# A rebuilt attention stage ahead of a branched expert stage, with the first two conditional blocks prepared before the branch

## The chip, the cores and the metric

The kernel runs on one core of a Trainium2 chip. The metric is the device time of one launch in microseconds (us). The kernel before takes 843.26 us, the median of three runs (842.16 to 844.25). All arithmetic is fp32.

## What is computed

Two parts are chained. The first is cross attention between a sequence and a small state, in both directions; the second sends each row of the result through one of eight experts, the one whose embedding it is closest to.

```python
# x: (8, 8, 512, 64), state: (8, 8, 32, 64)       B, H, S, D and Ns = 32
scores = scale * x @ state.T                      # softmax over the 32 states
xread  = softmax(scores) @ state                  # 512 rows a head
scores2 = scale * state @ x.T                     # softmax over the 512 positions
sread  = softmax(scores2) @ x                     # 32 rows a head
rows = concat(xread, sread) as (8*544, 8*64)      # N = 4352 rows of D = 512
xn, en = rows / |rows|, emb / |emb|
logits = xn @ en.T / tau                          # 8 experts
e, gate = argmax(logits), softmax(logits)[argmax]
out = gate * relu(rows @ w1[e]) @ w2[e]           # w1: 512x1024, w2: 1024x512
```

## The kernel before, in words

**Attention stage.** A *unit* is one batch `b` and one half `g` of its heads (four heads), 16 units in all, numbered `u = 2b + g`. `states(b)` puts the state of a batch block-diagonally into `bdst` (four copies on POOL), transposes it on PE (`st_ps`), copies it to `bd` and multiplies it with the normalised expert embeddings (`pj_ps`), so that eight extra columns of `bdst` give the router's logits along with the read. `scores(u)` transposes `x` on PE (`xt_ps`, eight 128x128 blocks), multiplies it with the state twice: once as `sT_ps` (states on the partitions, 512 positions along the row; for the softmax over positions) and once as `s_ps` (positions on the partitions; for the softmax over states). The first softmax makes `e2` and a diagonal matrix `dg` of reciprocal sums, the second makes `e1`. `reads(u)` transposes `e1` (`a_ps`) to `aT`, multiplies `e2` by `dg` while it turns it (`e_ps`) to `a2`, and then makes the two reads, `x_ps` (from `aT`) and `sr_ps` (from `a2`). `rows(b)` writes the rows to DRAM (`x_rows`), adds the logits, squares the rows for their norm (four `junk` activations a batch), and `choose` finds the expert. After each four batches `state_rows` does the same for the state rows (`xst_ps`, `lg_ps`). In the loop over units, `scores(u+1)` stands ahead of `reads(u)`.

The loads of `x` (1 MB a batch, in pieces of 256 bytes, four issues of 256 KB) and of the first expert weights `w1` (2 MB each, all eight kept in `w1_sb`), and the writes of the rows, are all issued by SP. A load of `x` for batch `b+2` waits until the two buffers' older batch is read.

**Routing.** Counts, ranks and destinations of the rows are worked out on DVE and with some matmuls (`rk_ps`, `inv_ps`), 207 to 243 us. The result is a table of blocks of 128 rows of one expert each.

**Expert stage.** `run(a, z)` goes over the blocks `j`: `gather` (POOL, an indirect load of 128 rows), `turn_x` (PE transposes to `xT`), `hidden` (PE with `w1`, relu to `h`), `turn_h` (`hT`), `result` (PE with `w2`, scaled by the gate to `y`, an indirect store by POOL). `load_w2` is issued by SP. There are always 34 blocks; up to 41 can be needed, by the data. So `run(0, 34)` is followed by two nested branches, for blocks 34 to 36 and 37 to 40. The count is read into a register of every engine. In these runs 37 blocks are used, so the first branch is entered and the second is not. Inside a branch `run` begins anew, with gathers, transposes and first weights.

**What sets the order.** A scheduler orders the instructions of each engine when the program is built, by priorities that follow the code and its own estimate of when each is ready; on the chip each engine runs its list in that order, one after the other.

The few lines that set the order of the units are

```python
ready = {0: scores(0, 0, x_nat[0], st[0][1])}
for u, (b, g) in enumerate(units):
    ...
    if u + 1 < len(units):
        ready[u + 1] = scores(b1, g1, x_nat[b1], st[b1][1])
    reads(b, g, x_nat[b], st[b][0], xr[b], *ready.pop(u))
```

## Time and profile before

| what | us |
|---|---|
| median of three runs | 843.26 |
| the profiled execution, its own time | 844.45 |
| its span, first to last instruction | 842.4 |
| attention stage, span 0 to the end of the last `sr_ps` | 206.8 |
| routing, to the first `h_ps` | 206.8 to 253.8 |
| 34 blocks, to the end of the last `y_ps` ahead of the branch | 253.8 to 771.3 |
| PE without work at the branch | 771.3 to 781.2 |
| three conditional blocks and the end | 781.2 to 842.4 |

Engines are PE (matmul), PEld (its weight load, which overlaps), DVE, ACT, POOL and SP. A group of instructions is named by its line, the tile it writes and the tiles it reads. An fp32 matmul appears as two instructions, an fp32 transpose as one; so `sT_ps` x4 is two matmuls. PE is busy for 91% of the span, DVE for 27%, ACT for 16% and POOL for 14%, but these are averages over a stage in which DVE and ACT work most of the time (attention) and one in which they mostly wait (experts).

### The profile page before, as it was taken

The page shows a single profiled execution, that of the slowest core. Times are in us where ns is not written, and L with a number is a line of the kernel's source. Part 1 is how long each engine was busy: PE and PEld are TensorE (multiplying, and loading weights), DVE is VectorE, ACT ScalarE, POOL GpSimd, SP SyncE. Part 2 cuts the span into 40 slices and gives each one's busy share as a digit, 9 for nine tenths or more (in the row PEclk, how much of TensorE's full clock was granted, in tenths as well). Part 3 has the DMA queues.
Part 4 walks back from the last instruction along what each step waited for, and adds up shares of the span by engine and source line. Part 5 has one row for each costly group of instructions (what it writes and reads, how often), then busy time and mean ns, then how long its engine had stood idle before and what let it go on. Part 6 is the DMA issues. An engine that isn't in the chain of part 4 may idle for free.

```text
span 842.4 us, 8400 instructions
## 1 busy us (share of the span) xinstructions
PE 769.3 (91%) x3104; PEld 438.0 (52%) x3104; DVE 225.6 (27%) x499; ACT 133.7 (16%) x272; POOL 115.9 (14%) x184
## 2 busy tenths in 40 slices
PE   6899999998359999999999999999999999996994
PEld 4677767777244454454444544545445454442441
DVE  3455555555701111121121211212112111111111
ACT  3244444344100010000000000001000010000000
POOL 2011111101211101111111101111111110002000
PEclk9899999999559999999999999999999999999897
DMA  9486662242033464553644545546455464446130
GB/s 264 186 279 181 211 216 81 47 102 79 9 130 143 137 217 146 165 204 132 209 164 152 203 138 191 178 140 220 140 176 198 130 212 140 149 179 212 50 113 16
DMA packets 92753, 131.40 MB, mean 156 GB/s; under 512 B 37726, under 2 KB 45918, under 8 KB 92712
## 3 DMA queue, kind: packets, MB, share of 16 engines
q1 hardware_dynamic: 86760, 112.20, 41.3%
q0 software_dynamic: 5920, 18.62, 6.4%
q8 instruction: 27, 0.44, 0.2%
q14 instruction: 14, 0.11, 0.0%
q10 hardware_dynamic: 32, 0.02, 0.0%
HBM read 113.00 MB, written 18.61 MB: 156 GB/s over the span
## 4 chain that ended last, share of the span: by engine, by line
PE 82%; issue 7%; DVE 5%; DMA 2%; POOL 1%; ACT 1%; POOLq 0%; ACTq 0%; DVEq 0%
PE y_ps L516 28%; PE h_ps L490 28%; PE sT_ps L219 5%; PE ht_ps L509 3%; PE s_ps L224 3%; PE x_ps L271 3%; PE sr_ps L279 3%; PE xt_ps L479 2%; PE inv_ps L431 2%; PE e_ps L264 2%; DVE xT L70 1%; PE pj_ps L199 1%; DMA xin<-x_rows,src_row 1%; PE a_ps L259 1%; DMA x_rows<-xs 1%
## 5 line engine op out<-in xcount | busy, mean ns | idle before, releaser
L516 PE MATMUL y_ps<-w,hT 128*128 128x512 f32 x592 | 263.9, 599 | 1.1 <-ACT hT L68 0.8
L490 PE MATMUL h_ps<-w_sb,xT 128*128 x592 | 262.6, 597 | 0.0
L490 PEld LDWEIGHTS h_ps<-w_sb,xT 128*128 128x128 f32 x592 | 113.4, 192 | 142.6 <-issue 142.3
L516 PEld LDWEIGHTS y_ps<-w,hT 128*128 128x128 f32 x592 | 109.4, 190 | 129.2 <-issue 123.9
L498 ACT ACTIVATE h<-h_ps 128x512 f32<-128x512 f32 x37 | 22.1, 597 | 431.9 <-PE h_ps L490 431.9
L520 DVE TENSOR_SCALAR y<-y_ps,gpos 128x512 f32<-128x512 f32 x37 | 27.8, 751 | 227.8 <-PE y_ps L516 227.8
L500 DVE TENSOR_SCALAR h<-h_ps 128x512 f32<-128x512 f32 x37 | 25.6, 692 | 231.2 <-PE h_ps L490 231.2
L521 POOL DMA_INDIRECT out_dram<-y,dst_row x37 | 37.5, 1014 | 312.0 <-DVE y L520 304.7
L466 POOL DMA_INDIRECT xin<-x_rows,src_row x37 | 38.1, 1030 | 217.9 <-PE xt_ps L479 199.4
L219 PE MATMUL sT_ps<-xT,bd 128*128 128x512 f32 x64 | 39.4, 745 | 7.4 <-DVE xT L70 7.2
L509 PEld LDWEIGHTS ht_ps<-ident,h 128*128 128x128 f32 x296 | 34.6, 141 | 19.5 <-issue 19.5
L68 ACT ACTIVATE hT<-ht_ps 128x512 f32<-128x512 f32 x37 | 22.1, 597 | 129.9 <-PE ht_ps L509 129.9
L479 PE MATMUL xt_ps<-ident,xin 128*128 128x128 f32 x148 | 24.1, 290 | 20.3 <-DMA xin<-x_rows,src_row 20.3
L509 PE MATMUL ht_ps<-ident,h 128*128 128x128 f32 x296 | 38.4, 273 | 0.0
L224 PEld LDWEIGHTS s_ps<-bd,xT 128*128 128x128 f32 x256 | 32.0, 194 | 10.0 <-issue 10.0
L271 PE MATMUL x_ps<-bdst,aT 128*128 128x264 f32 x128 | 32.9, 401 | 0.0
L279 PEld LDWEIGHTS sr_ps<-xn,a 128*32 128x32 f32 x512 | 29.0, 110 | 5.5 <-DVE r L249 4.5
L279 PE MATMUL sr_ps<-xn,a 128*32 128x64 f32 x512 | 31.6, 220 | 0.0
L481 DVE COPY xT<-xt_ps 128x512 f32<-128x512 f32 x37 | 25.2, 682 | 21.6 <-PE xt_ps L479 21.6
L224 PE MATMUL s_ps<-bd,xT 128*128 128x64 f32 x256 | 30.5, 272 | 0.0
L479 PEld LDWEIGHTS xt_ps<-ident,xin 128*128 128x128 f32 x148 | 18.3, 150 | 22.0 <-DMA xin<-x_rows,src_row 11.4
L252 POOL TENSOR_TENSOR e<-e,r 128x512 f32<-128x512 f32 x16 | 16.8, 1048 | 78.3 <-DVE r L251 62.6
(128 smaller groups left out, 474.3 us busy)
## 6 DMA issues: line engine op xcount, KB each, us to landing
w<-in_moe_w_dram SPq DMA_DIRECT2D x37, 2048.0 KB, 10.1
w_sb<-in_moe_w_dram SPq DMA_DIRECT2D x8, 2048.0 KB, 9.4
xn<-in_x_dram SPq DMA_DIRECT2D x32, 256.0 KB, 4.1
x_rows<-xr SPq DMA_DIRECT2D x16, 512.0 KB, 5.5
xin<-x_rows,src_row POOLq DMA_INDIRECT x37, 3.7
out_dram<-y,dst_row POOLq DMA_INDIRECT x37, 7.8
...
```

The lines of the kernel that those rows point to most:

```text
L219: nc.tensor.matmul(sT, lhsT=bd[:, g, j], rhs=xT[:, j], start=(j == 0), stop=(j == 1))
L224: nc.tensor.matmul(s[:, c * P + j * half : c * P + j * half + half], lhsT=xT[:, j, c * P : c * P + P], rhs=bd[:, g, j, j * half : j * half ...
L271: nc.tensor.matmul(ps[:, 0:XW], lhsT=aT[:, c * P : c * P + P], rhs=bs[:, g], start=True, stop=True)
L279: nc.tensor.matmul(ps[q0 : q0 + Ns, i * Dh : i * Dh + Dh], lhsT=a2[:, c * P + i * Ns : c * P + i * Ns + Ns], rhs=xn[:, c, (HPG * g + i) * ...
L466: nc.gpsimd.indirect_dma_start(out=t, out_offset=None, in_=x_rows[:], in_offset=bass.IndirectOffsetOnAxis(ap=src_row[:, j : j + 1], axis=0 ...
L479: nc.tensor.transpose(ps[:, k * P : k * P + P], t[:, k * P : k * P + P], ident)
L490: nc.tensor.matmul(ps, lhsT=xT[:, k * P : k * P + P], rhs=w1f[:, ds(ek * (KD * F) + k * F + i * 512, 512)], start=(k == 0), stop=(k == KD ...
L500: nc.vector.tensor_scalar(dst, ps, 0.0, None, ALU.max)
L509: nc.tensor.transpose(ps[:, k * P : k * P + P], h[:, f0 : f0 + P], ident)
L516: nc.tensor.matmul(ps, lhsT=hT[:, k * P : k * P + P], rhs=w2[:, k], start=(k == 0), stop=(k == KF - 1))
L520: nc.vector.tensor_scalar(y, ps, gpos[:, j : j + 1], None, ALU.mult)
L521: ins = nc.gpsimd.indirect_dma_start(out=out[:], out_offset=bass.IndirectOffsetOnAxis(ap=dst_row[:, j : j + 1], axis=0), in_=y, in_offset= ...
```

## The change

The attention stage is rebuilt; eight things differ.

1. **State, prepared once.** The transposed states of all batches (`bd`, two tiles of four batches) and the products with the embeddings (`proj`) are made at the start, from two copies of the state that ten issues on ACT's queue load (1 MB together). `states(b)` then only issues four small loads of the state straight into `bdst` (SP) and copies `proj` (POOL).
2. **`sT_ps` in two halves.** Each matmul writes 64 of the 128 partitions, with 64 columns of `bd`.
3. **No `s_ps`.** The scores with positions on the partitions come from `sT_ps` by a DVE transpose of 32x32 blocks (`STREAM_TRANSPOSE`), the subtraction of the maximum moves from DVE to POOL.
4. **No `a_ps`.** `e1` is turned to `aT` by a second DVE transpose.
5. **`dg` is gone.** ACT scales `e2`, and `e_ps` is a plain transpose.
6. **Copies move to ACT:** `a2`, and all four `xr` copies of a unit.
7. **Order of the units.** `turn(u+2)` (the transposes of `x`) stands ahead of `reads(u)`, and `scores(u+2)` behind it. `x` of three batches is kept: the third buffer, `spare`, and one of the `bd` tiles lie in the space of the last expert's `w1`.
8. **The branch.** `run(0, 34)` also gathers and turns blocks 34 and 35 and hands the turned blocks to `run(34, 37, xT)`, which gathers only block 36 anew. The register read of the count stands ahead of `run(0, 34)` in the code.

The diff, without most of the start and the plain renamings:

```diff
         def load_x(b):
-            t = att.tile([P, NCH, D], FP32, tag="xn", name="xn")
+            if b % 3 == 2:
+                t = spare[:, 0 : NCH * D].rearrange("p (c d) -> p c d", c=NCH)
+            else:
+                t = att.tile([P, NCH, D], FP32, tag="xn", name="xn")
...
+        for b in range(B):
+            p0 = Ns * (b % 4)
+            nc.scalar.dma_start(st_row[p0 : p0 + Ns, b // 4], state[b].rearrange("h n d -> n h d"))
...
+            nc.scalar.dma_start(
+                st_nat[g], state[:, HPG * g : HPG * g + HPG].rearrange("b i n d -> (i n) b d")
+            )
         x_nat = {0: load_x(0)}
...
         nc.scalar.dma_start(emb, moe_expert_emb[:])
...
         x_nat[1] = load_x(1)
+        x_nat[2] = load_x(2)
...
         def states(b):
             bs = bdst[b % 2]
             for i in range(HPG):
-                nc.gpsimd.tensor_copy(
-                    bs[Ns * i : Ns * i + Ns, :, Dh * i : Dh * i + Dh], st_nat[Ns * i : Ns * i + Ns, b]
-                )
-            ps = bank("st_ps")
-            for g in range(HG):
-                for j in range(2):
-                    nc.tensor.transpose(
-                        ps[:, (2 * g + j) * P : (2 * g + j + 1) * P], bs[:, g, j * P : j * P + P], ident
-                    )
-            bd = att.tile([P, HG, 2, P], FP32, tag="bd", name="bd")
-            nc.scalar.activation(bd.rearrange("p g j n -> p (g j n)"), ps, AF.Copy)
-            pp = bank("pj_ps")
-            for g in range(HG):
-                for j in range(2):
-                    nc.tensor.matmul(
-                        pp[:, g * E : g * E + E], lhsT=bd[:, g, j], rhs=enT[:, 2 * g + j],
-                        start=(j == 0), stop=(j == 1),
-                    )
-            nc.vector.tensor_copy(
-                bs[:, :, GW:XW], pp[:, 0 : HG * E].rearrange("p (g e) -> p g e", e=E)
-            )
-            return bs, bd
-        def scores(b, g, xn, bd):
-            xT = att.tile([P, 2, S], FP32, tag="xT", name="xT")
+                nc.sync.dma_start(
+                    bs[Ns * i : Ns * i + Ns, :, Dh * i : Dh * i + Dh],
+                    state[b].rearrange("(g i) n d -> i n g d", g=HG)[i],
+                )
+            nc.gpsimd.tensor_copy(bs[:, :, GW:XW], proj[:, b])
+            return bs
+        def turn(b, g, xn):
+            xT = [att.tile([P, S], FP32, tag="xT", name="xT", bufs=3) for _ in range(2)]
             for j in range(2):
                 ps = bank("xt_ps")
                 h0 = HPG * g + 2 * j
                 for c in range(NCH):
                     nc.tensor.transpose(ps[:, c * P : c * P + P], xn[:, c, h0 * Dh : h0 * Dh + P], ident)
-                copy((nc.vector, nc.scalar)[j], xT[:, j], ps)
+                copy((nc.vector, nc.scalar)[j], xT[j], ps)
+            return xT
+        def scores(b, g, xT):
             sT = bank("sT_ps")
             for j in range(2):
-                nc.tensor.matmul(sT, lhsT=bd[:, g, j], rhs=xT[:, j], start=(j == 0), stop=(j == 1))
-            s = bank("s_ps")
-            half = 2 * Ns
-            for j in range(2):
-                for c in range(NCH):
-                    nc.tensor.matmul(
-                        s[:, c * P + j * half : c * P + j * half + half],
-                        lhsT=xT[:, j, c * P : c * P + P],
-                        rhs=bd[:, g, j, j * half : j * half + half],
-                        start=True, stop=True,
-                    )
+                o = j * 2 * Ns
+                nc.tensor.matmul(
+                    sT[o : o + 2 * Ns], lhsT=bd[b // 4][:, b % 4, 2 * g + j], rhs=xT[j], start=True, stop=True
+                )
             r2 = att.tile([P, 3], FP32, tag="r2", name="r2")
-            e2 = att.tile([P, S], FP32, tag="e2", name="e2")
-            dg = att.tile([P, P], FP32, tag="dg", name="dg")
+            e2 = att.tile([P, S], FP32, tag="e2", name="e2", bufs=3)
             nc.vector.tensor_reduce(r2[:, 0:1], sT, axis=AX, op=ALU.max)
             nc.vector.tensor_scalar(r2[:, 0:1], r2[:, 0:1], -SCALE, None, ALU.mult)
+            nrb = S // Ns
+            shp = [P, nrb, Ns]
+            r1 = att.tile([P, 2, nrb], FP32, tag="r1", name="r1")
+            e1 = att.tile([P, nrb, Ns], FP32, tag="e1", name="e1")
+            e1f = e1.rearrange("p c n -> p (c n)")
+            nc.vector.transpose(e1f, sT)
             nc.scalar.activation(e2, sT, AF.Exp, bias=r2[:, 0:1], scale=SCALE, accum_out=r2[:, 1:2])
+            nc.vector.tensor_reduce(r1[:, 0].unsqueeze(2), e1, axis=AX, op=ALU.max)
+            nc.gpsimd.tensor_tensor(e1, e1, bc(r1[:, 0], shp, 2), ALU.subtract)
+            nc.scalar.activation(e1, e1, AF.Exp, scale=SCALE)
             nc.vector.tensor_scalar(r2[:, 1:2], r2[:, 1:2], 1e-9, None, ALU.add)
             nc.vector.reciprocal(r2[:, 2:3], r2[:, 1:2])
-            nc.vector.tensor_scalar(dg, ident, r2[:, 2:3], None, ALU.mult)
-            nch = NCH * HPG
-            shp = [P, nch, Ns]
-            r1 = att.tile([P, 2, nch], FP32, tag="r1", name="r1")
-            e1 = att.tile([P, nch, Ns], FP32, tag="e1", name="e1")
-            s3 = s.rearrange("p (c n) -> p c n", n=Ns)
-            nc.vector.tensor_reduce(r1[:, 0].unsqueeze(2), s3, axis=AX, op=ALU.max)
-            nc.vector.tensor_tensor(e1, s3, bc(r1[:, 0], shp, 2), ALU.subtract)
-            nc.scalar.activation(e1, e1, AF.Exp, scale=SCALE)
+            nc.scalar.activation(e2, e2, AF.Copy, scale=r2[:, 2:3])
             nc.vector.tensor_reduce(r1[:, 1].unsqueeze(2), e1, axis=AX, op=ALU.add)
             nc.vector.tensor_scalar(r1[:, 1], r1[:, 1], 1e-9, None, ALU.add)
             nc.vector.reciprocal(r1[:, 1], r1[:, 1])
             nc.gpsimd.tensor_tensor(e1, e1, bc(r1[:, 1], shp, 2), ALU.mult)
-            return e1.rearrange("p c n -> p (c n)"), e2, dg
-        def reads(b, g, xn, bs, xr, e1, e2, dg):
-            ps = bank("a_ps")
-            for c in range(NCH):
-                nc.tensor.transpose(ps[:, c * P : c * P + P], e1[:, c * P : c * P + P], ident)
-            aT = att.tile([P, S], FP32, tag="aT", name="aT", bufs=1)
-            nc.scalar.activation(aT, ps, AF.Copy)
+            aT = att.tile([P, S], FP32, tag="aT", name="aT", bufs=3)
+            nc.vector.transpose(aT, e1f)
+            return aT, e2
+        def reads(b, g, xn, bs, xr, aT, e2):
             ps = bank("e_ps")
             for c in range(NCH):
-                nc.tensor.matmul(
-                    ps[:, c * P : c * P + P], lhsT=e2[:, c * P : c * P + P], rhs=dg, start=True, stop=True
-                )
+                nc.tensor.transpose(ps[:, c * P : c * P + P], e2[:, c * P : c * P + P], ident)
             a2 = att.tile([P, S], FP32, tag="a2", name="a2", bufs=1)
-            nc.vector.tensor_copy(a2, ps)
+            nc.scalar.activation(a2, ps, AF.Copy)
             for c in range(NCH):
                 ps = bank("x_ps")
                 nc.tensor.matmul(
                     ps[:, 0:XW], lhsT=aT[:, c * P : c * P + P], rhs=bs[:, g], start=True, stop=True
                 )
-                copy((nc.vector, nc.scalar)[c % 2], xr[:, c, g], ps[:, 0:XW])
+                nc.scalar.activation(xr[:, c, g], ps[:, 0:XW], AF.Copy)
...
         st = {0: states(0)}
         xr, xs = {}, {}
-        ready = {0: scores(0, 0, x_nat[0], st[0][1])}
+        ready = {u: scores(*units[u], turn(*units[u], x_nat[units[u][0]])) for u in range(2)}
         for u, (b, g) in enumerate(units):
             if g == 0:
+                if b + 1 < B:
+                    st[b + 1] = states(b + 1)
                 load_w1(b)
-                xr[b] = att.tile([P, NCH, HG, XW], FP32, tag="xr", name="xr")
+                xr[b] = att.tile([P, NCH * HG * XW], FP32, tag="xr", name="xr").rearrange("p (c g w) -> p c g w", c=NCH, g=HG)
                 if b % GB == 0:
                     xs[b // GB] = att1.tile([P, D], FP32, tag="xs", name="xs")
-            if u + 1 < len(units):
-                b1, g1 = units[u + 1]
-                ready[u + 1] = scores(b1, g1, x_nat[b1], st[b1][1])
-            reads(b, g, x_nat[b], st[b][0], xr[b], *ready.pop(u))
-            if g == 0 and b + 1 < B:
-                st[b + 1] = states(b + 1)
+            later = u + 2 < len(units)
+            if later:
+                b2, g2 = units[u + 2]
+                xT = turn(b2, g2, x_nat[b2])
+            reads(b, g, x_nat[b], st[b], xr[b], *ready.pop(u))
+            if later:
+                ready[u + 2] = scores(b2, g2, xT)
             if g == HG - 1:
-                if b + 2 < B:
-                    x_nat[b + 2] = load_x(b + 2)
+                if b + 3 < B:
+                    x_nat[b + 3] = load_x(b + 3)
...
-    def run(a, z):
-
-        xin = {j: gather(j) for j in range(a, min(a + 3, z))}
+    def run(a, z, xT=None, ahead=0):
+
+        xin = {j: gather(j) for j in range(a + 2 if xT else a, min(a + 3, z))}
         w2 = {j: load_w2(j) for j in range(a, min(a + 2, z))}
-        xT = {j: turn_x(xin.pop(j)) for j in range(a, min(a + 2, z))}
+        xT = xT or {j: turn_x(xin.pop(j)) for j in range(a, min(a + 2, z))}
         h = {a: hidden(a, xT.pop(a))}
         for j in range(a, z):
             if j + 1 < z:
                 h[j + 1] = hidden(j + 1, xT.pop(j + 1))
             hT = turn_h(h.pop(j))
-            if j + 3 < z:
+            if j + 3 < z + ahead:
                 xin[j + 3] = gather(j + 3)
-            if j + 2 < z:
-                xT[j + 2] = turn_x(xin.pop(j + 2))
+            if j + 2 < z + ahead:
+                xT[j + 2] = turn_x(xin.pop(j + 2), "xT" if j + 2 < z else "xTa")
             result(j, hT, w2.pop(j))
             if j + 2 < z:
                 w2[j + 2] = load_w2(j + 2)
+        return xT
+
 
 
     always = N // P
     more = always + (NBLK - always) // 2
-    run(0, always)
     blocks = nc.values_load(
         count[0:1, 0:1], min_val=always, max_val=NBLK,
         skip_runtime_bounds_check_because="the sum over the experts of their rows / 128, rounded up",
     )
+    xT = run(0, always, ahead=2)
     with tc.If(blocks > always):
-        run(always, more)
+        run(always, more, xT)
```

On PE a unit in the middle of the stage stood like this before (`x_ps` and `sr_ps` of one unit behind the `xt_ps`, `sT_ps` and `s_ps` of the next):

```order
L215 MATMUL xt_ps<-ident,xn 128x128 x8
L219 MATMUL sT_ps<-xT,bd 128x512 x2
L224 MATMUL s_ps<-bd,xT 128x64 x8
L259 MATMUL a_ps<-ident,e_354 128x128 x4
L264 MATMUL e_ps<-dg,e_345 128x128 x4
L271 MATMUL x_ps<-bdst_108,aT 128x264 x4
L279 MATMUL sr_ps<-xn,a_487 32x64 x16
```

and stands like this with the change (the `sT_ps` of unit 4, then the `xt_ps` of unit 5, the reads of unit 3 and the `sT_ps` of unit 5):

```order
L282 MATMUL sT_ps<-xT,w_sb 64x512 x2
L273 MATMUL xt_ps<-ident,w_sb 128x128 x8
L316 MATMUL e_ps<-ident,e_443 128x128 x4
L321 MATMUL x_ps<-bdst_123,aT 128x264 x4
L329 MATMUL sr_ps<-xn,a_586 32x64 x16
L282 MATMUL sT_ps<-xT,w_sb 64x512 x2
```

`s_ps` and `a_ps` are gone, and the `sT_ps` of a unit now stands behind the reads of an earlier one, with a whole group between it and the `x_ps` that needs it.

On DVE the second softmax of a unit before ran from its sum (L249) to its reciprocal (L251) with only copies between (`e1_354` and `r1_353` belong to one unit, `xr_213` to the unit ahead of it):

```order
L249 TENSOR_REDUCE r1_353<-e1_354 128x16
L70 COPY xr_213<-x_ps_376 128x264
L250 TENSOR_SCALAR r1_353<-r1_353 128x16
L70 COPY xr_213<-x_ps_382 128x264
L251 RECIPROCAL r1_353<-r1_353 128x16
L295 TENSOR_TENSOR lg_70<-xr_213 128x32
```

With the change the list of unit 6 (`r1_730`, `e1_731`) and unit 7 (`r2_800`, `e1_805`, `r1_804`) reads

```order
L335 COPY xs_313<-sr_ps_779 32x256
L288 TENSOR_REDUCE r2_800<-sT_ps_797 128x1
L304 TENSOR_REDUCE r1_730<-e1_731 128x16
L289 TENSOR_SCALAR r2_800<-r2_800 128x1
L296 STREAM_TRANSPOSE e1_805<-sT_ps_797 128x512
L305 TENSOR_SCALAR r1_730<-r1_730 128x16
L345 TENSOR_TENSOR lg_70<-xr_671 128x32
L298 TENSOR_REDUCE r1_804<-e1_805 128x16
L306 RECIPROCAL r1_730<-r1_730 128x16
L202 TENSOR_REDUCE lmax_71<-lg_70 128x4
L70 COPY xT_850<-xt_ps_852 128x512
```

The sum and the reciprocal of unit 6 now stand behind the first reading of `sT_ps` of unit 7 (L288). In four of the units 2 to 13 (3, 6, 8 and 11) the reciprocal stands behind that line, in unit 6 the sum too; unit 14 stands like unit 6.

At the branch PE's list read before

```order
L516 MATMUL y_ps<-w_3904,hT 128x512 x8
L509 MATMUL ht_ps<-ident,h 128x128 x8
L516 MATMUL y_ps<-w_3959,hT 128x512 x8
L554 TENSOR_LOAD count
L558 COMPARE_AND_BRANCH
L479 MATMUL xt_ps<-ident,xin 128x128 x8
L450 TENSOR_LOAD eblk
```

and with the change it reads

```order
L562 MATMUL ht_ps<-ident,h 128x128 x8
L532 MATMUL xt_ps<-ident,xin 128x128 x4
L569 MATMUL y_ps<-w_3735,hT 128x512 x8
L608 TENSOR_LOAD count
L613 COMPARE_AND_BRANCH
L503 TENSOR_LOAD eblk
```

Four of the eight transposes (`xt_ps`) stand between `ht_ps` and `y_ps` of block 33, the other four likewise in block 32, and the register read of the count is still next to the branch.

## Rows read from the trace of the kernel before

**Rows 1.** The page: PE's granted clock, tenths of full speed, in 40 slices.

```profile
PEclk9899999999559999999999999999999999999897
```

**Rows 2.** Timeline, units 1 and 15: start, us, engine, line, instructions.

```profile
43.41 1.97 PE L279 MATMUL sr_ps<-xn,a 128*32 128x64 f32 x32
...
45.32 1.09 PE L215 MATMUL xt_ps<-ident,xn 128*128 128x128 f32 x8
...
204.83 1.97 PE L279 MATMUL sr_ps<-xn,a 128*32 128x64 f32 x32
```

**Rows 3.** Chain that ended last, in order of time: start us, us, what.

```profile
63.92 0.89 PE e_ps L264 x8
64.81 1.90 PE x_ps L271 x8
66.71 1.92 PE sr_ps L279 x32
70.07 1.99 PE sT_ps L219 x4
...
82.80 3.57 PE sT_ps L219 x4
...
117.88 1.07 PE lg_ps L315 x8
```

**Rows 4.** Groups by line, 0 to 240: busy us, mean ns, idle before.

```profile
L298 ACT ACTIVATE junk<-xr 128x512 f32<-128x512 f32 x32 | 20.1, 627 | 0.6
...
L252 POOL TENSOR_TENSOR e<-e,r 128x512 f32<-128x512 f32 x16 | 16.8, 1048 | 78.3 <-DVE r L251 62.6 <-DVE r L235 15.2
...
L68 ACT ACTIVATE xr<-x_ps 128x264 f32<-128x264 f32 x32 | 12.5, 390 | 12.5 <-PE x_ps L271 11.1
L234 DVE TENSOR_REDUCE r<-sT_ps 128x1 f32<-128x512 f32 x16 | 11.1, 692 | 34.6 <-PE sT_ps L219 34.6
...
L236 ACT ACTIVATE e<-sT_ps,r 128x512 f32<-128x512 f32 x16 | 11.0, 688 | 45.1 <-DVE r L235 45.1
...
L248 ACT ACTIVATE e<-e 128x512 f32<-128x512 f32 x16 | 10.1, 631 | 7.9 <-DVE r L238 7.5 <-DVE e L247 0.4
...
L235 DVE TENSOR_SCALAR r<-r 128x1 f32<-128x1 f32 x16 | 2.4, 150 | 0.5
```

**Rows 5.** Busy time by stretch; last three: PE clock, DMA share, GB/s.

```profile
0.00:10.00 10.00, 2.95 (x15) 2.56 (x15) 1.87 (x9) 4.08 (x6) 5.92 (x35) 1.00 1.00 181
...
80.00:90.00 10.00, 9.19 (x51) 6.94 (x52) 3.50 (x9) 2.34 (x6) 0.00 (x0) 0.83 0.64 224
```

**Rows 6.** Timeline, the start.

```profile
1.26 9.59 SPq L105 DMA_DIRECT2D xn<-in_x_dram  x8
...
3.01 0.63 ACT L131 ACTIVATE junk<-emb 8x512 f32<-8x512 f32 x1
...
6.36 0.56 PE L139 MATMUL en_ps<-ident,emb 8*128 8x8 f32 x4 [6.36 <-DVE emb L136]
...
8.65 1.87 PE L199 MATMUL pj_ps<-enT,bd 128*128 128x8 f32 x8 [0.69 <-ACT bd L195]
...
10.38 1.95 PE L215 MATMUL xt_ps<-ident,xn 128*128 128x128 f32 x8
...
26.83 2.53 PE L271 MATMUL x_ps<-bdst,aT 128*128 128x264 f32 x8
```

**Rows 7.** Timeline, around the branch.

```profile
747.65 7.03 PE L490 MATMUL h_ps<-w_sb,xT 128*128 x16
...
764.16 7.13 PE L516 MATMUL y_ps<-w,hT 128*128 128x512 f32 x16 [0.30 <-ACT hT L68]
...
781.22 2.18 PE L479 MATMUL xt_ps<-ident,xin 128*128 128x128 f32 x8 [9.93 <-DMA xin<-x_rows,src_row]
...
783.19 15.23 PE L490 MATMUL h_ps<-w_sb,xT 128*128 x32
```

**Rows 8.** Chain that ended last, POOL at the branch.

```profile
772.12 0.51 POOLq L554
```

75 lines of the change are left out of this document (66 added, 9 removed).

## The prediction

> **What bounds the kernel now.** I read the chain of waits first. In it PE work follows PE work through the whole attention stage [rows 3] and again through the expert blocks; other engines stand in it at the start, in routing, at the branch and at the end. So the stage is worth what PE's list costs, as long as nobody else becomes later than PE. The timeline gives the stage's rate [rows 2]: the `sr_ps` of unit 1 ends at 43.41 + 1.97 = 45.4 us, that of unit 15 at 204.83 + 1.97 = 206.8, so 14 units take 161.4 us, or 11.5 each. The groups by line [rows 4] show the prices of the DVE, ACT and POOL steps and that DVE and ACT wait for PE, not PE for them. PE's granted clock [rows 1] is full but for the start, routing and a few dips. The second place is the branch [rows 7]: the last `y_ps` ahead of it ends at 764.16 + 7.13 = 771.3, and the first `h_ps` behind it starts at 783.2.
>
> **A unit after the change, on PE.** Eight transposes 1.09 [rows 2]; `e_ps`, now four passes instead of eight, half of 0.89; `x_ps` 1.90, `sr_ps` 1.92, `sT_ps` 1.98 [rows 3]. Sum 7.3 us. `s_ps`, `a_ps`, and the transposes and products of each batch's state are gone. Small differences at the edges of pieces I leave in.
>
> **Is another engine longer?** ACT gets, with the durations of [rows 4]: two softmax exponentials (0.69 and 0.63), four wide copies or scalings at 0.63 as bound (`xT`, `e2`, `a2`, and one more for its accumulator reads), four `xr` copies at 0.39, and two squares a unit at 0.63: 6.7 us. DVE: six wide steps at 0.69 (two reductions of scores, one sum, one `xT`, two block transposes), 4.2 us, and short ones of about 0.15. POOL: two of 1.05. The block transpose has no row. Its floor is a short step, 0.15; its ceiling would be the DVE list filling the unit, (7.3 - 2.8 - 1.5) / 2 = 1.5. I take 0.69, the reduction over the same 128x512 scores. So PE stays longest, ACT close behind.
>
> **Do the results arrive in time?** From the end of a unit's `sT_ps` to its `aT` there are: maximum 0.69, block transpose 0.69, second maximum 0.69, POOL subtraction 1.05, exponential 0.63, sum 0.69, two short steps 0.3, POOL product 1.05, block transpose 0.69 [rows 4]: 6.5 us, and some 0.1 for each of nine hand-overs, 7.4. PE reaches that unit's `x_ps` one whole unit and the transposes later: 7.3 + 1.09 + 0.45 = 8.8. The chain fits, by 1.4 us, if no engine's list holds it up. It does in units 3, 6, 8, 11 and 14, where DVE's list has the reciprocal behind the first look at the next unit's `sT_ps`. Count from the end of that later `sT_ps`; PE wants `x_ps` 1.5 after it.
> - Units 3, 8, 11: maximum 0.69, block transpose 0.69, short steps 0.4, POOL product 1.05, transpose 0.69: 3.6, so 2.1 late each.
> - Unit 6: also the sum stands behind, and the next unit's second maximum (0.69 each) goes ahead, after which POOL does that unit's subtraction (1.05) first: 6.1, so 4.6 late.
>
> Units 2 to 13: 12 x 7.3 = 87.6, and 3 x 2.1 + 4.6 = 10.9. `state_rows` once in the middle costs PE its transposes, a wait and `lg_ps` (1.07 [rows 3]), 2.3. The clock: in four of the eight batches before, a `sT_ps` ran long, 3.57 instead of 1.98 [rows 3], where the granted clock falls from full speed (2.4 GHz) to half (1.2): the stretch around it has a mean of 0.83 [rows 5]. I keep two such, 3.2. Units 14 and 15 have no next unit to cover them: `sT_ps` 1.98, then `x_ps` of 14 at 6.1, `sr_ps` to 9.9, `x_ps` of 15 and `sr_ps` to 14.2, 16.2 together. Sum 87.6 + 10.9 + 2.3 + 3.2 + 16.2 = 120.2 against 161.4: **41.2 less**.
>
> **The start.** Before, the embeddings' chain is done by 6.4 and PE goes on [rows 6]. Now their load stands on ACT's queue behind ten issues of state (1 MB in pieces of 256 bytes), while SP issues 3 MB of `x`. In the first 10 us the DMA engines are already full at 181 GB/s [rows 5] with `x` (eight issues from 1.26 on [rows 6]). If the two queues share them, 1 MB takes 2 x 1.05 / 0.181 = 11.6 us and the embeddings land at 13.5; if state goes first, 5.8 and about 8. The former is nearer to the row, which shows no room. The Trainium skill (Trainium Kernel Development and Optimization, section Key Constraints) says that queues of different engines run on the same 16 DMA engines and interleave; by that rule it is the former, and no row here shows two full queues at once to agree or not; without it the start would be some 5 us shorter. Behind the embeddings: norm and scaling to PE as before, 6.4 - 3.0 = 3.4; a second set of eight small transposes and its copies 2.5; 16 transposes at 1.95 for eight, 3.9; a copy 0.7; eight matmuls at twice 1.87, 3.7; `xt_ps` 1.95, a copy, and the first `sT_ps` at the low clock [rows 6, 3]. That gives 33.9, `aT` of unit 0 by 42, `x_ps` of unit 0 to 44.5 (2.53 at the low clock), and then `sr_ps`, `sT_ps`, `xt_ps`, `e_ps`, `x_ps` and `sr_ps`: unit 1 ends at about 53.5. **8 more** (bounds: 3 with state first, 12 with all of it at the low clock).
>
> **The branch.** Gone are the wait for the gather, 9.9, and the eight transposes, together 783.2 - 771.3 = 11.9. The first two blocks' `h_ps` took 15.23, against twice 7.03 in the steady part [rows 7], so 1.2 more were lost to a start at the lower clock. The transposes that move go into `ht_ps` to `y_ps` of blocks 32 and 33, where PE waits 0.30 for `hT` anyway [rows 7]; in the other blocks they stand there already, and I cost them nothing. Gathers of blocks 34 and 35 are issued a block earlier by an idle POOL. The register read of the count is still next to the branch on PE: 0.51 on POOL [rows 8], so I charge 0.5 (bounds: 0, as PE's list runs ahead of its matmuls, and 9.9, if the code behind the branch comes as late as the gather did). **12.6 less.** Routing and the 34 blocks stay.
>
> **The sum** is made against the profiled execution: 842.4 - 41.2 + 8 - 12.6 = 796.6 span, and 844.45 - 842.4 = 2.05 around it, 798.7. The profiled execution is 1.2 above the median of 843.26, so I say 797 us.
>
> **The rivals.**
> - *PE alone decides.* The lists hold nothing up, no dip, state first: 87.6 + 2.3 + some 12 for the last two units is 102, 59.5 less; with 3 and 12.6: 774. For it: the chain fits by 1.4. Against: the list of unit 6. 15%.
> - *The halves of `sT_ps` run side by side.* Nothing of the kind is in the trace: there each `sT_ps` uses all columns, and the `sr_ps` of a batch all write the same 32 partitions. If PE saved 0.99 of 1.98, ACT's 6.7 would bound the unit: 0.6 x 12 = 7 less than the case above, 767. The Trainium skill (TensorEngine Tiling (Array Packing), section Key Properties) says that different tiles of the array work in parallel; by that rule this is what two 64-column halves do. 5%, since it needs the first case as well.
> - *The low clock through the stage.* PE waits more often than before. At 1.2 GHz the unit is 1.95 for eight transposes, half of that for four, 2.5, 1.9 and 3.6: 10.9 [rows 6, 3], which hides the late results: 12 x 10.9 + 2.3 + 18 = 151, 10 less; with 8 and 12.6: 828. For it: the dips come with PE at work [rows 3, 5]; against: full clock in most slices [rows 1]. 11%.
> - *Loads of `x` come late.* A batch's 1 MB takes 5.8 us at 181 GB/s and is issued two units (14.6) before use, but behind 2 MB of `w1` and the rows. If the five later ones are 4 us late each: 817. 6%.
> - *The branch gives nothing.* PE finds the code or a register late: up to 10 back, 807. 6%.
> - *Slower: every unit waits, and cold.* If each unit's `aT` is as late as unit 6's (lists in an order that the chip never catches up with), a unit is 7.3 + 4.6 = 11.9; if the waits also drop the clock, 3.6 more, 15.5: 12 x 15.5 + 2.3 + 16 = 204, 43 more, with 8 and 12.6: 881. It decides from 12.3 a unit: 12 x 12.3 + 18.3 = 166 = 161.4 - 8 + 12.6. For it: five lists of sixteen have the flaw; against: the others don't. 4%.
>
> **How the numbers follow.** My forecast has 53%. Its own bounds: start 3 to 12, late results half or double, branch 3 to 13.1, so about 785 to 815. The range of 768 to 820 takes in the first case, the late loads and the branch, and leaves out the side-by-side halves, the low clock and the slower case, 20%. All cases but the last are faster by far more than 0.3% (2.5 us, about what a measurement of this kernel can tell from no change): faster 0.95, same 0.01, slower 0.04.
>
> **What would show it.** In the new profile: `sr_ps` of unit 1 near 53.5 and of unit 15 near 174; about 7.3 us between the `sr_ps` of units 4 and 5, 9 to 12 at units 3 and 6 with PE waiting for `aT`; `STREAM_TRANSPOSE` near 0.69; no gap over 1 us at the branch; the embeddings' square on ACT near 13.5. I am wrong if PE waits for `a2` or `xr` (ACT bound), if the transposes take over 1.5, if the low clock holds, or if PE stands still at the branch.

## The result, and the profile after the change

The changed kernel takes **801.66 us** (median of 4 runs, 801.46 to 802.44) against 842.98 (842.16 to 844.25, 4 runs): ratio 0.951, 95% interval 0.949 to 0.953, so 41 us faster. The profiled execution took 801.46, span 799.7 (before 842.4), 42.7 less. The forecast was 797 with a range of 768 to 820.

| place | before | forecast | after |
|---|---|---|---|
| end of `sr_ps` of unit 1 | 45.4 | 53.5 | 53.5 |
| from there to the end of `sr_ps` of unit 15 | 161.4 | 120.2 | 124.1 |
| from there to the end of the last `y_ps` ahead of the branch | 564.5 | as before | 564.4 |
| from there to the end of the span | 71.1 | 58.5 | 57.7 |

Differences: +8.1, -37.3, -0.1 and -13.4, together -42.7. The sum holds; inside it, terms of opposite sign were off.

**The clock** on the page of the changed kernel (tenths of full speed in 40 slices), to set beside [rows 1]:

```profile
PEclk9989879985589999999999999999999999999997
```

Full speed again in most slices, but more dips in the attention stage (slices 3 to 9).

**The start**, timeline of ACT, then of PE (start us, us, engine, line, operation, [idle before <- what ended it]), to set beside [rows 6]:

```profile
0.76 7.27 ACTq L122 DMA_DIRECT2D begin<-in_state_dram  x8
...
11.29 2.26 ACTq L130 DMA_DIRECT2D begin<-in_moe_expert_emb_dram  x1
18.25 0.63 ACT L144 ACTIVATE junk<-begin 8x512 f32<-8x512 f32 x1 [3.04 <-DMA begin<-in_moe_expert_emb_dram]
```

```profile
21.56 0.56 PE L152 MATMUL en_ps<-ident,begin 8*128 8x8 f32 x4 [21.56 <-DVE begin L149]
...
27.28 2.52 PE L243 MATMUL pj_ps<-begin 128*128 128x64 f32 x16
...
51.52 1.97 PE L329 MATMUL sr_ps<-xn,a 128*32 128x64 f32 x32
```

The embeddings' load is only issued at 11.3, since ACT's list reaches it behind the ten loads of state, and lands at 18.2; the forecast was 13.5. What follows was costed too dear (`pj_ps`, eight matmuls and x16 in the row, at 2.52, not 3.7; `xt_ps` at 1.05, not 1.95), so that 53.5 came out by two errors. The first 10 us by window (start:end, length, busy time of PE, PEld, DVE, ACT and POOL, then PE's granted clock, DMA share, GB/s), to set beside [rows 5]:

```profile
0.00:10.00 10.00, 0.00 (x0) 0.00 (x0) 2.66 (x7) 0.00 (x0) 3.46 (x27) 1.00 1.02 176
```

With both queues at work the DMA engines moved 176 GB/s, no more than the 181 of before, when `x` had them nearly alone. So the two queues did share what one had; whether that is also what makes the ten issues take until 11.3 no run separates: most issues take 0.3 to 0.5 us with pauses between them, and the embeddings' own takes 2.26 here and 0.63 at the head of the list (run 5).

**The units**, timeline of PE, to set beside [rows 2, 3]: a clean unit (from `sr_ps` to the next `sr_ps`), then what stands ahead of units 3, 6, 8 and 11.

```profile
121.00 1.97 PE L329 MATMUL sr_ps<-xn,a 128*32 128x64 f32 x32
122.91 1.08 PE L282 MATMUL sT_ps<-xT,bd 128*64 128x512 f32 x4
123.92 1.09 PE L273 MATMUL xt_ps<-ident,w_sb 128*128 128x128 f32 x8
124.85 0.60 PE L316 MATMUL e_ps<-ident,e 128*128 128x128 f32 x4
125.28 1.95 PE L321 MATMUL x_ps<-bdst,aT 128*128 128x264 f32 x8
127.16 1.97 PE L329 MATMUL sr_ps<-xn,a 128*32 128x64 f32 x32
...
65.03 2.95 PE L321 MATMUL x_ps<-bdst,aT 128*128 128x264 f32 x8 [2.45 <-DVE r L301]
...
90.86 3.89 PE L321 MATMUL x_ps<-bdst,aT 128*128 128x264 f32 x8 [4.32 <-DVE r L302]
...
113.39 1.88 PE L365 MATMUL lg_ps<-enT,xsT 128*128 128x8 f32 x8 [8.05 <-DVE xsT L362]
115.12 1.95 PE L273 MATMUL xt_ps<-ident,w_sb 128*128 128x128 f32 x8
...
140.59 3.42 PE L321 MATMUL x_ps<-bdst,aT 128*128 128x264 f32 x8 [2.44 <-DVE r L301]
```

From `sr_ps` to `sr_ps` a clean unit takes 127.16 - 121.00 = 6.16 us (forecast 7.3): `sT_ps` is 1.08 instead of 1.98. Units 3, 6 and 11 wait for `aT` as forecast, and behind each wait `x_ps` takes 2.95 to 3.89 instead of 1.95. By window, around the wait in `state_rows`:

```profile
110.00:120.00 10.00, 6.61 (x26) 6.10 (x27) 3.42 (x14) 3.17 (x8) 1.97 (x6) 0.52 0.86 300
```

The clock is 0.52 of full speed, nearly all of it at the lower of the two levels (2.4 and 1.2 GHz). Over 6.15 for a clean unit, unit 3 takes 4.3 more, unit 6 7.4, unit 8 (with `state_rows`) 13.1, unit 11 4.3, the other eight 3.6 (1.2 of it unit 5, where `x_ps` waits 0.77, and 1.5 unit 13, whose two `sT_ps` stand apart); with 12 x 6.15 and 17.6 for units 14 and 15 that is the 124.1.

Over the whole stretch PE is busy for 149.4 of 161.4 us before and for 100.0 of 124.1 after. So the 37.3 us are 49.3 less of work on PE, the half clock included, and 12.0 more of waiting. No run puts `s_ps` and `a_ps` back, so what each pass that is gone gives by itself isn't shown, but for the halves of `sT_ps` (run 3).

**The branch**, timeline of PE, to set beside [rows 7]: there is no gap now, and the two `h_ps` take 13.90 instead of 15.23.

```profile
734.88 7.13 PE L569 MATMUL y_ps<-w,hT 128*128 128x512 f32 x16
741.85 13.90 PE L543 MATMUL h_ps<-w_sb,xT 128*128 x32
```

**The block transpose**, groups by line (busy us, mean ns | idle before):

```profile
L309 DVE STREAM_TRANSPOSE aT<-e 128x512 f32<-128x512 f32 x16 | 11.3, 709 | 9.2 <-POOL e L307 9.1
```

It takes 0.71 (forecast 0.69; no row of before had it).

### The profile page after: what moved, and what is told of

The parts are those of the page before. It is cut to its first block, busy times and chain, and to the rows that moved or that the text cites. A ratio compares the mean times of both kernels' runs of the same rounds, so it can differ in the third digit from the quotient of the medians.

```text
span 799.7 us, 7569 instructions
## 1 busy us (share of the span) xinstructions
PE 709.1 (89%) x2664; PEld 385.2 (48%) x2664; DVE 215.7 (27%) x457; ACT 146.6 (18%) x319; POOL 123.8 (15%) x176
## 3 DMA queue, kind: packets, MB, share of 16 engines
q10 hardware_dynamic: 4288, 1.07, 0.8%
## 4 chain that ended last, share of the span: by engine, by line
PE 79%; DVE 7%; issue 6%; DMA 3%; POOL 2%; ACT 1%; POOLq 0%; ACTq 0%; DVEq 0%
PE y_ps L569 30%; PE h_ps L543 29%; PE x_ps L321 5%; PE sr_ps L329 4%; PE ht_ps L562 4%; PE xt_ps L532 2%; PE inv_ps L484 2%; PE sT_ps L282 1%; DMA begin<-in_state_dram 1%; DMA xin<-x_rows,src_row 1%; DMA begin<-in_moe_expert_emb_dram 1%; PE xt_ps L273 1%; POOL e L307 1%; DVE r L288 1%; DVE r L304 1%
## 5 line engine op out<-in xcount | busy, mean ns | idle before, releaser
L519 POOL DMA_INDIRECT xin<-x_rows,src_row x37 | 38.1, 1028 | 229.6 <-PE xt_ps L532 211.7
L321 PE MATMUL x_ps<-bdst,aT 128*128 128x264 f32 x128 | 41.1, 477 | 17.1 <-DVE r L301 4.9
L321 PEld LDWEIGHTS x_ps<-bdst,aT 128*128 128x128 f32 x128 | 28.6, 234 | 24.5 <-issue 5.7
L70 DVE COPY hT<-ht_ps 128x512 f32<-128x512 f32 x37 | 25.6, 692 | 7.2 <-PE ht_ps L562 5.9
L329 PEld LDWEIGHTS sr_ps<-xn,a 128*32 128x32 f32 x384 | 23.8, 117 | 5.5 <-ACT xr L324 3.1
L484 PE MATMUL inv_ps<-rr,oh 128*128 128x82 f32 x68 | 14.8, 422 | 13.0 <-POOL rr L477 13.0
L329 PE MATMUL sr_ps<-xn,a 128*32 128x64 f32 x384 | 25.8, 229 | 0.0
L324 ACT ACTIVATE xr<-x_ps 128x264 f32<-128x264 f32 x64 | 21.7, 389 | 10.9 <-PE x_ps L321 10.6
```

Source lines behind the costliest of these rows:

```text
L70: eng.tensor_copy(dst, src)
L321: nc.tensor.matmul(ps[:, 0:XW], lhsT=aT[:, c * P : c * P + P], rhs=bs[:, g], start=True, stop=True)
L329: nc.tensor.matmul(ps[q0 : q0 + Ns, i * Dh : i * Dh + Dh], lhsT=a2[:, c * P + i * Ns : c * P + i * Ns + Ns], rhs=xn[:, c, (HPG * g + i) * ...
L484: nc.tensor.matmul(inv_ps[:, 0 : 2 * NBLK], lhsT=oh[:, s], rhs=rr[:, s].rearrange("p t k -> p (t k)"), start=(s == 0), stop=(s == NSLOT - 1),)
L519: nc.gpsimd.indirect_dma_start(out=t, out_offset=None, in_=x_rows[:], in_offset=bass.IndirectOffsetOnAxis(ap=src_row[:, j : j + 1], axis=0 ...
```

## The experiments

The kernel before was timed beside every run (medians 842.5 to 843.0), so medians are set beside each other; "the stretch" is from the end of `sr_ps` of unit 1 to that of unit 15 (124.1 in the changed kernel).

**1. The branch part undone.**

```diff
-    xT = run(0, always, ahead=2)
+    run(0, always)
...
-        run(always, more, xT)
+        run(always, more)
```

(and in `run` itself the gathers and transposes of the first two blocks begin at `a` again)

> The changed kernel with its branch part undone: the first two conditional blocks are gathered and transposed behind the branch again; the attention part stays. If the two traces are read rightly, the end of the last y_ps ahead of the branch to the end of the span is 71 us again instead of 57.7, and the time is 801.7 + 13.4 = 815 us; PE waits about 10 us for the gather and the two h_ps take 15.2. Rival: the branch part gave its 13 us only because attention now leaves PE or the queues in another state; then the gap comes back in part and the time is 803 to 810.

Measured: 814.37 us, ratio 0.965 (0.962 to 0.969), 12.7 above the changed kernel.

```profile
753.40 2.18 PE L532 MATMUL xt_ps<-ident,xin 128*128 128x128 f32 x8 [9.99 <-DMA xin<-x_rows,src_row]
755.37 14.64 PE L543 MATMUL h_ps<-w_sb,xT 128*128 x32
```

The wait for the gather is back as before [rows 7], and so is 0.74 of the 1.33 by which the two `h_ps` were slower there; the stretch (123.7) is not touched. The branch part is worth 12.7, by itself.

**2. One unit ahead instead of two.**

```diff
-        ready = {u: scores(...) for u in range(2)}
+        ready = {u: scores(...) for u in range(1)}
...
-            later = u + 2 < len(units)
+            later = u + 1 < len(units)
```

(and `u + 1` in the two places that read `units` and write `ready`)

> The changed kernel with scores one unit ahead of reads instead of two; everything else as it is. Theory: the attention part is fast because a unit's softmax has a whole unit of PE work to hide in. With one unit ahead, PE has only eight transposes and e_ps (1.5 us) between sT_ps and the x_ps that needs its result 7.4 to 9 us later, so a wait of 6 to 7.5 us stands in each unit, and x_ps behind it takes 3 to 3.9 instead of 1.95: a unit of 12.5 to 16 us instead of 7 to 8, 65 to 125 us more in all, 865 to 925 us, slower than the kernel before. Rival: it is fast because PE has fewer passes and the softmax is shorter; then most of the gain stays, below 830 us.

Measured: 893.11 us, ratio 1.059 (1.056 to 1.063), slower than before. One unit in PE's timeline:

```profile
75.00 1.09 PE L273 MATMUL xt_ps<-ident,w_sb 128*128 128x128 f32 x8
78.78 1.12 PE L316 MATMUL e_ps<-ident,e 128*128 128x128 f32 x4 [2.69 <-ACT e L303]
82.65 3.89 PE L321 MATMUL x_ps<-bdst,aT 128*128 128x264 f32 x8 [2.75 <-DVE aT L309]
```

PE waits for `e2` and again for `aT` in every unit but the one behind `state_rows`, and `x_ps` takes 3.5 to 3.9: the stretch is 208.0, or 14.9 a unit. So fewer passes on PE without cover lose 50 us against the kernel before. This is the slower rival of the prediction (15.5 a unit, 881 us): its mechanism is real, and the second unit of look-ahead is what keeps it away. The run does not give the kernel before with fewer passes: there `scores(u+1)` stood ahead of `reads(u)`, so that the reads of one unit covered the softmax of the next, and here they stand ahead of it.

**3. Halves of `sT_ps` over the full width.** Each half's 64 columns of state get 64 columns of zeros beside them, and the two passes add up.

```diff
-                    sT[o : o + 2 * Ns], lhsT=bd[b // 4][:, b % 4, 2 * g + j], rhs=xT[j], start=True, stop=True
+                    sT, lhsT=bd[b // 4][:, b % 4, g, o : o + P], rhs=xT[j], start=(j == 0), stop=(j == 1)
```

> The changed kernel with each half of sT_ps as a pass over all 128 output partitions (64 columns of state beside 64 columns of zeros, added up in PSUM) instead of a pass over 64. Theory: the two 64-column halves run side by side in the changed kernel, which is why a sT_ps takes 1.08 there. Then sT_ps is 1.98 here and a unit 0.9 longer: up to 14 x 0.9 = 12.6 more, less what the waits of four units hide, so 808 to 815 us. Rival: a pass costs what it does whatever its width, and the 1.98 of the kernel before had another cause; then sT_ps stays near 1.08 and the time near 802.

Measured: 804.18 us, ratio 0.954 (0.951 to 0.957), 2.5 above the changed kernel: less than either the 6 to 13 expected, yet not the rival.

```profile
128.47 1.97 PE L330 MATMUL sr_ps<-xn,a 128*32 128x64 f32 x32
130.37 1.98 PE L283 MATMUL sT_ps<-xT,bd 128*128 128x512 f32 x4
...
135.38 1.97 PE L330 MATMUL sr_ps<-w_sb,a 128*32 128x64 f32 x32
```

`sT_ps` is 1.98 again and a clean unit 6.91, so two 64-column halves do run side by side in the changed kernel. There a half that stands alone (the scheduler put transposes between the two once) takes as long as the pair:

```profile
152.24 1.07 PE L282 MATMUL sT_ps<-xT,bd 128*64 128x512 f32 x2
153.24 0.77 PE L273 MATMUL xt_ps<-ident,xn 128*128 128x128 f32 x5
```

The Trainium skill's rule (TensorEngine Tiling (Array Packing), section Key Properties) that different tiles of the array work in parallel agrees with the trace: 1.08 for the pair here, 1.07 for one half. But the 0.9 that PE saves in each unit is worth only 2.5 us in all, and the 95% intervals of the two ratios overlap (0.951 to 0.957 and 0.949 to 0.953). In the run the longest wait ahead of an `x_ps` is 3.2 instead of 4.8, and all `x_ps` together take 38.1 instead of 41.2. That the longer unit covers the late results better is argued from this: the built lists changed too, and the waits stand in other units (4, 7, 12 and 15).

**4. Filling the waits.** Transposes that nobody reads, ahead of `x_ps` in units 3, 6, 11 and 14.

```diff
+            n = {3: 8, 6: 16, 11: 8, 14: 16}.get(HG * b + g, 0)
+            if n:
+                fill = bank("fill_ps")
+                for i in range(n):
+                    nc.tensor.transpose(fill[:, P * (i % 4) : P * (i % 4) + P], ident, ident)
```

> The changed kernel with transposes that nobody reads put on PE into the waits of units 3, 6, 11 and 14 (8, 16, 8 and 16 of them, each about 0.27 us, ahead of x_ps). Theory: x_ps takes 2.95 to 3.89 there instead of 1.95, and sr_ps up to 2.9 instead of 1.95, because the granted clock has fallen to half while PE stood still. Then with PE busy x_ps is back near 1.95, and the time falls by 5 to 9 us, to 793 to 797. Rival: x_ps runs long because ACT's copies of it come late or DVE hands over aT in pieces; then x_ps stays as it is and the time is 801 to 805.

Measured: 796.58 us (793.34 to 801.64), ratio 0.943 (0.939 to 0.947), 5.1 below the changed kernel, although nothing comes earlier from DVE. The profiled run is the slowest of the four, since in it the start ran at half clock; its stretch is 118.8.

```profile
66.32 1.04 PE L321 MATMUL fill_ps<-ident 128*128 128x128 f32 x8
68.93 2.02 PE L326 MATMUL x_ps<-bdst,aT 128*128 128x264 f32 x8 [1.57 <-DVE r L301]
...
88.66 1.91 PE L321 MATMUL fill_ps<-ident 128*128 128x128 f32 x16
93.20 2.68 PE L326 MATMUL x_ps<-bdst,aT 128*128 128x264 f32 x8 [2.63 <-issue]
```

A transpose cost half of what I took, so the fill left 1.6 to 3.0 of each wait. Still `x_ps` of units 3 and 11 is 2.02 again. By window around unit 11, the changed kernel and then this run, the granted clock goes from 0.83 to 1.00:

```profile
140.00:150.00 10.00, 9.41 (x63) 7.12 (x64) 6.01 (x16) 6.46 (x17) 2.38 (x4) 0.83 0.96 315
140.00:150.00 10.00, 8.43 (x69) 6.33 (x68) 7.04 (x19) 7.33 (x20) 3.96 (x5) 1.00 1.03 335
```

So the slow `x_ps` is the clock behind PE's wait, and neither ACT's copies nor `aT` in pieces. The clock does not fall behind every such wait: of the nine waits of 2.2 to 2.5 without fill ahead of `x_ps` of units 3 and 11 (the changed kernel, runs 1, 5, 6 and the copy alone of run 8), seven have a slow `x_ps` and two have 2.02.

**5. Embeddings ahead of the state on ACT's queue.** The two loads of `emb` and `tau` are moved up, ahead of the loop over the state.

> The changed kernel with the loads of the embeddings and of tau ahead of the ten loads of state on ACT's queue. Theory: PE's first work starts at 21.6 us because the embeddings stand behind the state's issues and land at 18.2; the embeddings' own square should then run at about 3 us, and PE begin with the state's transposes when state has landed, at 11 to 16 us. The time is 5 to 9 us less, 793 to 797. Rival: the state loads, the first x or the low clock bind right behind; PE's scores of unit 0 then move by less than 3 us and the time is 799 to 802.

Measured: 792.32 us, ratio 0.941 (0.936 to 0.945), 9.3 less. ACT's timeline:

```profile
1.74 7.84 ACTq L126 DMA_DIRECT2D begin<-in_state_dram  x8
...
12.05 1.28 ACT L144 ACT_TABLE_LOAD   x1 [12.05 <-DMA begin<-in_state_dram]
13.34 0.63 ACT L144 ACTIVATE junk<-begin 8x512 f32<-8x512 f32 x1
```

A little more than forecast, but not as forecast: the square runs at 13.3, 4.9 earlier, not at 3. Its data is there (in the kernel before the same load, also issued at 0.76, let it run at 3.0), but ACT's list is still at its loads until 12.05. `sr_ps` of unit 1 ends at 47.85, 5.6 earlier; the stretch is 120.1, 4.0 less, with less of it at half clock (`x_ps` 38.6 in all instead of 41.2). Of the 4.0, unit 6 gives 3.2 (its wait is 2.30 instead of 4.32) and unit 11 1.6, where after the same wait of 2.44 `x_ps` takes 2.02 instead of 3.42. Why, I can't say.

**6. The first `lg_ps` one unit later.**

```diff
-                    state_rows(b // GB)
+                    held = state_rows(b // GB)
+            if held and (not later or g < HG - 1):
+                state_logits(*held)
+                held = None
```

(`state_logits` is `state_rows` from `lg_ps` on)

> The changed kernel with the product lg_ps of the first state_rows put one unit later in the program (behind the reads and scores of unit 8), so that PE need not wait for the copy xsT. Theory: PE's 8.05 us before lg_ps is DVE's copy xsT standing behind the softmax of unit 9 in DVE's list, and lg_ps, xt_ps, e_ps and x_ps behind it take 3 us longer at half clock. The wait goes, but the late result of unit 8 (its reciprocal stands behind the next maximum) is no longer hidden: 2.1 to 2.5 comes back, with some low clock. Net 5 to 8 us less, 794 to 797. Rival: xsT is late because the state rows themselves are; then PE waits for them wherever lg_ps stands, and the time is 800 to 802.

Measured: 795.44 us, ratio 0.945 (0.941 to 0.950), 6.2 less.

```profile
109.99 2.02 PE L321 MATMUL x_ps<-bdst,aT 128*128 128x264 f32 x8 [1.87 <-ACT junk L348]
...
115.97 1.06 PE L369 MATMUL lg_ps<-enT,xsT 128*128 128x8 f32 x8
```

The wait of 8.05 is gone and `lg_ps` costs 1.06; 1.87 comes back ahead of unit 8's `x_ps` (the row names ACT, but `aT` of that unit lands at 109.89, just ahead of it). That and the time are as forecast. Further on the waits move as well, which was not forecast: unit 11 waits no more, and `x_ps` of unit 12 waits 4.37.

**7. Each maximum behind the reciprocal before it.** This tries my reason for the late units: the reciprocal behind the next unit's maximum.

```diff
-            nc.vector.tensor_reduce(r2[:, 0:1], sT, axis=AX, op=ALU.max)
+            with (tc.issue_after(recip[-1]) if recip else ExitStack()):
+                nc.vector.tensor_reduce(r2[:, 0:1], sT, axis=AX, op=ALU.max)
```

> The changed kernel with one thing set in DVE's list: a unit's maximum over sT_ps stands behind the reciprocal of the unit before, in all units. Theory: the waits of units 3, 6, 11 and 14 (2.45, 4.32, 2.44 and 4.77 us) come from the reciprocal that stands behind the next unit's maximum. They go or shrink to under 1 us, and x_ps and sr_ps behind them run at full clock: 9 to 16 us less, 786 to 793. Rival: the chain from sT_ps to aT is too long for its cover whatever the list, so the waits move to other units; then the time is 797 to 803.

Measured: 804.61 us (801.52 to 808.67), ratio 0.955 (0.950 to 0.959): a miss, 3 above the changed kernel, with intervals that overlap, so no gain and no sure loss. The waits don't go, they spread over ten units, 1.2 to 3.2 each. Unit 4, timeline of all engines:

```profile
72.94 0.42 DVE L338 COPY xs<-sr_ps 32x256 f32<-32x256 f32 x1 [2.68 <-PE sr_ps L332]
...
73.39 0.69 DVE L307 TENSOR_REDUCE r<-e 128x16 f32<-128x512 f32 x1
...
74.72 1.05 POOL L310 TENSOR_TENSOR e<-e,r 128x512 f32<-128x512 f32 x1 [3.46 <-DVE r L309]
...
75.80 0.71 DVE L312 STREAM_TRANSPOSE aT<-e 128x512 f32<-128x512 f32 x1 [0.51 <-POOL e L310]
...
76.57 2.05 PE L324 MATMUL x_ps<-bdst,aT 128*128 128x264 f32 x8 [1.19 <-DVE aT L312]
```

The copy of `sr_ps` waits for PE 2.68 us at the head of DVE's list, and the sum behind it, whose input is long there, waits too. PE then waits for work that waited for PE.

**8. The copy alone, and copy and maximum together.** The copy into `xs` is issued behind the next unit's reciprocal; in the second kernel each maximum as well, as in 7.

```diff
+            with tc.issue_after(nxt):
+                nc.vector.tensor_copy(xs[b // GB][q0 : q0 + Ns, g * GW : g * GW + GW], ps[q0 : q0 + Ns, 0:GW])
```

> The copy of sr_ps into xs behind the reciprocal of the next unit, and the maxima left where they are. Theory: in units 3, 6, 11 and 14 the reciprocal stands behind the copy and behind the next maximum, which waits for sT_ps, 1.1 us later still; without the copy the maximum alone holds it as long, less 0.3. So the four waits stay within 0.5 of 2.4 and 4.3 us and the time is 799 to 802. Rival: the copy alone makes them; then they go, and the time is 788 to 795.

> The edit of each maximum behind the reciprocal before it, and beside it DVE's copy of sr_ps into xs of a unit set behind the reciprocal of the next unit. New theory, from the run with the maximum alone: the copy xs waits for the end of sr_ps and stands ahead of the next unit's sum in DVE's list, so sum, reciprocal, POOL's product and aT start only when PE has done sr_ps, and PE waits 1.2 to 3 us a unit for work that waited for PE. With both behind, the sum runs as soon as its exponential is there, and the waits ahead of x_ps shrink to 0 to 0.7: 9 to 14 us less than the changed kernel, 788 to 793. Old rival: the chain of DVE, ACT and POOL is itself longer than a unit of PE (6.3 us); then the waits only move once more, and the time is 798 to 806.

Measured: the copy alone 802.26 us, ratio 0.951 (0.948 to 0.954), no change, as expected; both 800.34 (796.67 to 802.05), ratio 0.949 (0.945 to 0.954), 1.3 less and inside the spread, the rival's value. Unit 11 of the second kernel:

```profile
136.38 0.69 DVE L70 COPY xT<-xt_ps 128x512 f32<-128x512 f32 x1 [0.95 <-PE xt_ps L273]
...
136.99 0.24 DVE L309 RECIPROCAL r<-r 128x16 f32<-128x16 f32 x1
...
138.45 0.71 DVE L312 STREAM_TRANSPOSE aT<-e 128x512 f32<-128x512 f32 x1
...
139.31 3.67 PE L324 MATMUL x_ps<-bdst,aT 128*128 128x264 f32 x8 [2.10 <-DVE aT L312]
```

Now a third copy that waits for PE (`xT`) stands ahead of the reciprocal. From the end of that unit's `sT_ps` (129.2) to `aT` (139.2) it is 10 us. PE covers some 7.6 without a wait (in the changed kernel, from the end of the `sT_ps` at 122.91 to the end of the `e_ps` ahead of the next `x_ps` but one, 131.6).

**9. Edits together.** First 5, 6 and 7; then 5, 6, 7 and the copy.

> The three edits together: embeddings first, each maximum behind the reciprocal before it, lg_ps one unit later. If the three costs are apart from each other the gains add, up to the late result of unit 8, which the second edit removes as well: 5 to 9, 9 to 16 and 8 to 10, so 767 to 779 us. Rival: with the waits gone ACT's list binds (6.7 us of it in a unit of 6.3 on PE), and half of the gain of the second edit is lost: 779 to 787.

> All four edits together: embeddings first, lg_ps one unit later, each maximum and each copy of sr_ps behind the reciprocal before it. If the last two together gain 9 to 14, the time is 787.5 less that, 773 to 779. Rival, the chain of the other engines binds: 784 to 790, no better than without the copy moved.

Measured: 787.47 us, ratio 0.938 (0.930 to 0.945), and 784.99, ratio 0.932 (0.929 to 0.935); both short of what was hoped for, both at about the rivals' values. 801.7 - 9.3 - 6.2 = 786: if the gains of the embeddings and of `lg_ps` add up, the order of DVE's list gives nothing that can be told. No run has these two edits alone, so the 786 is a sum and not a measurement.

**10. Three units ahead**, with 5 and 6, no order forced on DVE, one buffer more for `aT`, `e2`, `r1` and `r2`, and room made for them by laying `bd` of batches 4 to 7 into the idle weights too.

```diff
-            later = u + 2 < len(units)
+            later = u + 3 < len(units)
...
-                ready[u + 2] = scores(b2, g2, xT)
+                ready[u + 3] = scores(b2, g2, xT)
```

> Embeddings first and lg_ps one unit later, as measured before (these two alone would be 801.7 - 9.3 - 6.2 = 786), and scores three units ahead of reads instead of two, with a buffer more for aT, e2 and the short columns; no order forced on DVE. Theory: the chain from sT_ps to aT, in lists that make DVE wait for PE now and then, takes up to 10 us, and two units ahead leave it 7.6; three leave it about 14. Then all waits for aT ahead of x_ps go, whatever the order of DVE's list, and with them the x_ps and sr_ps at half clock: 13 to 19 us less, 767 to 773. Rival: another engine is itself longer than PE's unit of 6.3 us; then PE waits on, only for other things (aT, a2 or xr), and the time is 779 to 786.

Measured: **777.86 us** (775.63 to 782.15, 5 runs), ratio 0.923 (0.920 to 0.925): the fastest of all, 8 below the sum of 786 and 7 below the fastest run measured before it (784.99), where 13 to 19 were expected. PE's timeline:

```profile
41.31 1.95 PE L321 MATMUL x_ps<-bdst,aT 128*128 128x264 f32 x8
...
67.17 1.08 PE L282 MATMUL sT_ps<-xT,w_sb 128*64 128x512 f32 x4 [2.56 <-ACT xT L68]
...
119.15 3.04 PE L329 MATMUL sr_ps<-w_sb,a 128*32 128x64 f32 x32 [2.10 <-ACT a L318]
...
133.44 1.98 PE L282 MATMUL sT_ps<-xT,w_sb 128*64 128x512 f32 x4 [2.63 <-DVE xT L70]
```

No `x_ps` waits any more. The stretch is 104.9, but one more unit of scores now lies ahead of it, so it can't be set beside the 124.1. What is left are waits for the copies `xT` and `a2`, which now stand in ACT's and DVE's lists behind softmax, router and squaring work that is not urgent. So forecast and rival each have a part, and the time lies between their ranges.

## Why the prediction was right, and where its steps were not

- **The branch** (-12.6): right, -13.4 between the profiles and 12.7 by run 1. No gap stands at it, so the 0.5 charged for the register read is not seen.
- **A unit on PE** (7.3): mis-sized, 6.15. The term is `sT_ps`, 1.98 forecast and 1.08 measured, 0.9 of the 1.15; I gave halves side by side 5% because I tied them to a case without waits. As a mechanism they are there (run 3), as time they are worth 2.5 by that run, hardly clear of the noise.
- **Late results** (units 3, 8 and 11: 2.1 each, unit 6: 4.6): the places and sizes are right, 2.45, 2.44 and 4.32, and unit 8's stands hidden in `state_rows` until run 6 uncovers it (1.87). Unit 5, counted as clean, waits 0.77. The reason I gave, the next maximum alone, falls with runs 7 and 8: whichever instruction that waits for PE (maximum, copy of `sr_ps`, copy of `xt_ps`) comes first, it holds the softmax's tail, and with all that the chain is up to 10 us long, not 7.4. More cover (run 10) ends these waits, another order doesn't.
- **`state_rows`** (2.3): mis-sized, 10.4 from `xst_ps` (104.68) to the `xt_ps` behind `lg_ps` (115.12). I had costed PE's own steps and a short wait, and not looked where the copy `xsT` stands in DVE's list. Run 6 gives 6.2 of it back.
- **The clock** (3.2): mis-sized. Beyond the waits themselves, units 3, 6, 8 and 11 lose 29.1 - 9.2 (waits for `aT`) - 10.4 = 9.5, of which 7.7 is `x_ps` and `sr_ps` at half clock behind a wait and 1.3 `xt_ps` and `e_ps` of unit 8. I had carried the dips over by their number, as in four of eight batches before [rows 3, 5], and had not asked what PE does right after each wait I forecast. Run 4 shows that the clock behind the waits is the cause in units 3 and 11. That the dips of before come with PE at work was not a full reading: all four long `sT_ps` there stand right behind a wait of PE for `xT` of 0.35 to 0.68 us, though others of that length had none.
- **The start** (+8): right in sum, wrong inside: embeddings 4.7 later than forecast, the rest faster. I weighed when the bytes would land, and left out ACT's list: its issues take until 12 us, and ACT can do nothing else meanwhile (run 5). That the queues share the DMA engines is borne out (176 GB/s with both); how much of ACT's time comes from that stays open.
- **The slower rival** (4%): run 2 shows it to be one unit of look-ahead away, with 14.9 a unit where it said 15.5.

In the stretch the errors are -13.8 (twelve units), +8.1 (`state_rows`), +6.3 (clock) and +3.3 (the rest), together the 3.9 between 120.2 and 124.1. That 13.8 too much and 17.7 too little nearly cancel is luck, and so is the start: the time was right to 4.7 us, the account less so.
